# One kind of DMA at a time: transposes and GpSimd loads that wait for each other, in a Nyströmformer attention and SiLU layer kernel

## The chip, the core and the metric

One NeuronCore of a Trainium2 chip runs the whole program. The metric is the device time in microseconds of one execution. PE is TensorE, ACT ScalarE, DVE VectorE, POOL GpSimd, SP SyncE. PE has two clock levels, 1.2 and 2.4 GHz; the profile gives the granted clock as a share of the higher.

## The reference

Inputs q, k and v are 8 batches x 8 heads x 576 tokens x 64, in f32. Per head, 32 landmarks are means of 18 tokens each; three softmaxes follow, and an inverse by six Newton steps:

```python
q_lm = q.reshape(B, H, 32, 18, D).mean(axis=3)   # k_lm likewise
A = sm(q, k_lm); Bm = sm(q_lm, k_lm); C = sm(q_lm, k)
Z = Bm.transpose(0, 1, 3, 2) / (norm1(Bm) * norminf(Bm) + 1e-06)
for _ in range(6):
    Z = 2 * Z - Z @ Bm @ Z
x = A @ Z @ C @ v            # heads side by side: 4608 x 512
h = x @ w_in                 # 512 x 2048
out = (h * sigmoid(h)) @ w_out
```

## The kernel before, in words

The work goes batch by batch (8 batches, b = 0 to 7). A batch is cut into two groups of four heads (g = 0, 1), so that the 128 partitions hold four heads x 32 landmarks. What happens to one batch:

- **Loads** (`load_qk`, L361, and `load_v`, L369). k, q and v come from HBM in f32 and are cast to bf16 on the way, so GpSimd issues them (queue 0 of the profile): one DMA of 576 KB for k, one for q, three of 192 KB for v. Each of the tiles `qk` and `v` has two buffers.
- **Landmarks** (L504 to L515). From batch 2 on (`NPE = 2`), GpSimd adds up the 18 tokens in a tree, six instructions for k and six for q.
- **Transposes of q and k** (L470 to L477). Matmuls want head dimension on partitions. In batches 0 and 1 PE transposes; from batch 2 on the DMA does it: four `dma_start_transpose` per batch, `xt`, issued by SP (queue 1 of the profile), `qT<-qk`.
- **Softmaxes** (L535 to L688). Bm gives the Newton chain on DVE and PE; A gives `etn`; C gives `ce`. ACT computes all exponentials of a batch as one group, since it must change its function table between exp and SiLU.
- **Transposes of C** (L706 to L710). From batch 2 on two DMA transposes per batch, `ct<-ce`, also issued by SP. Then `cv` (L714) multiplies by v, `zt` and `m` (L743 to L771) fold in Z and w_in.
- **Layer 1** (`layer1`, L778): 16 blocks of two 512-column matmuls and two of sixteen 64-column ones, each followed by a SiLU on ACT. It writes `gm`, three buffers.
- **Layer 2** (`layer2`, L831): tiles of 16 matmuls of 512 columns, copied to `ost` (three buffers) by ACT or DVE, and stored by SP (`store_rows`, L857), on the same queue 1 as the transposes.

All instructions are put in order before the kernel is built: `Plan.run` (L59) simulates the five engines and one DMA queue with given durations, and takes at each free engine the ready operation of lowest `prio`. An operation with `dma=` us is queued behind the others on one modelled DMA (`dmaq`, L197) and is done `lag` later (1.9 us for loads, `XLAG` for transposes). What the plan yields is a fixed order for every engine; on the chip each engine goes through its list in order and waits where an operand isn't there yet. Stores and transposes stand in one list, SP's; loads and landmark additions in one list, POOL's. Nothing in the kernel before orders loads against transposes, except that a load into a `qk` buffer waits for the transposes that read that buffer two batches earlier (`p["qk_read"]`, L896), and v for `cv` two batches earlier (L897).

Of the kernel before, what the change touches and what calls it, by code (L numbers as in the profile page):

```python
# [17 lines left out]
class Op:  # L18


    def __init__(self, name, engs, emit, deps=(), prio=0.0, psum=0, cls=None, table=None,
                 tiled=False, dma=0.0, lag=None, group=None, crit=False):
        self.name, self.engs, self.emit, self.prio = name, engs, emit, prio
        self.deps = [d if isinstance(d, tuple) else (d, None) for d in deps if d is not None]
        self.psum, self.cls, self.table, self.tiled = psum, cls, table, tiled
        self.dma, self.lag, self.group, self.crit = dma, lag, group, crit
        self.unit = None
        self.margin = 0.0 if crit or engs[0][0] != "PE" else Plan.MARGIN
        self.slot = None
        self.readers = [0] * psum  # L30
        self.frees = []
        self.done = None
        self.left = 0
        self.users = []
# [218 lines left out]
def kernel(  # L253
# [9 lines left out]
    nc = tc.nc  # L263
# [11 lines left out]
    sc = 1.0 / float(Dh) ** 0.5  # L275
    SW = 128 + L
    NPE = 2
    XLAG = 3.5

    constp = ctx.enter_context(tc.tile_pool(name="constp", bufs=1))  # L280
    natp = ctx.enter_context(tc.tile_pool(name="natp", bufs=1))
# [66 lines left out]

    swdge = []

    def load(name, prio, us, issue, emit, deps=()):
        d = list(deps)
        if len(swdge) >= 8:
            d.append((swdge[-8], None))
        o = A(name, [("POOL", issue)], emit, d, prio, dma=us)
        swdge.append(o)
        return o

    qk_ops, v_ops, wi_ops, wo_ops = {}, {}, {}, {}

    def load_qk(b, prio, deps=()):  # L361
        for t, src in ((1, k), (0, q)):
            qk_ops[b, t] = load(
                f"ld{t}.{b}", prio + t * -0.1, 2.9, 0.75,
                lambda e, t=t, src=src: nc.gpsimd.dma_start(  # L365
                    out=qk_r[b % 2][:, t].rearrange("p g j d -> p g (j d)"),
                    in_=src[b].rearrange("(g h) (l j) d -> (h l) g (j d)", g=NG, l=L)), deps)

    def load_v(b, prio, deps=()):  # L369
        v_ops[b] = [load(  # L370
            f"ldv{a}.{b}", prio, 0.97, 0.6,
            lambda e, a=a: nc.gpsimd.dma_start(  # L372
                out=v_r[b % 2][a * L:(a + 1) * L, :, :],
                in_=v[b].rearrange("h (l a x) d -> a l h (x d)", l=L, a=VA)[a]), deps)
            for a in range(VA)]

    def load_w_in(f, prio):
# [53 lines left out]
    def attn(b):  # L431
# [12 lines left out]
        if on_pe:  # L444
            blocks = {}
            me["qk_read"] = []
            for t in (1, 0):
                todo = [(g, jp) for g in range(NG) for jp in range(JP)]
                for i in range(0, 18, 4):
                    part = todo[i:i + 4]  # L450

                    def tmm(e, t=t, part=part, key=(t, i)):
                        ps = bank(blocks[key])
                        for n, (g, jp) in enumerate(part):
                            mm(ps[:, n * 128:(n + 1) * 128],
                               qk[:, t, g, 2 * jp:2 * jp + 2, :].rearrange("p j d -> p (j d)"),
                               idb)
                    o = blocks[t, i] = A(f"tr{t}{i}.{b}", [("PE", mm_us(128, len(part)))], tmm,
                                         [qk_ops[b, t], cid], p0 + 7 + (1 - t) * 0.5, psum=1)
                    me["qk_read"].append(o)  # L460

                    def tcp(e, t=t, i=i, n=len(part), key=(t, i)):
                        copy(e, qT[:, t].rearrange("p g j x -> p (g j) x")[:, i:i + n, :],
                             bank(blocks[key])[:, 0:n * 128].rearrange("p (n x) -> p n x", x=128))
                    c = A(f"trc{t}{i}.{b}", either(128 * len(part)), tcp, [o], p0 + 8).reads(o)
                    for g, _ in part:
                        qt_ops.setdefault((t, g), []).append(c)
        else:
            me["qk_read"] = []
            for t in (1, 0):  # L470
                for g in range(NG):
                    qt_ops[t, g] = [A(
                        f"xt{t}{g}.{b}", [("SP", 0.1)],
                        lambda e, t=t, g=g: nc.sync.dma_start_transpose(  # L474
                            out=qT[:, t, g], in_=qk[:, t, g].rearrange("p j d -> p (j d)")),
                        [qk_ops[b, t]] + use, p0 + 5, dma=1.35, lag=XLAG)]
                    me["qk_read"] += qt_ops[t, g]  # L477


        lm_ops = {}  # L480
# [185 lines left out]
        for g in range(NG):  # L666
            ce, ct = ce_r[g], ct_r[g]

            def cm(e, g=g):
                for h in range(4):  # L670
                    for c in range(2):
                        mm(bank(me[f"C{g}"], c)[L * h:L * h + L, 0:HS],
                           lmT[64 * c:64 * c + 64, 0, g, L * h:L * h + L],
                           qT[64 * c:64 * c + 64, 1, g, :, L * h:L * h + L])
            me[f"C{g}"] = A(f"C{g}.{b}", [("PE", 0.24)], cm,
                            lmT_all + [(pb_op, -0.2)] + qt_ops[1, g], p0 + 18 + g,
                            psum=2, tiled=True)
            xs = []
            for c in range(2):
                def cx(e, g=g, ce=ce, c=c):  # L680
                    nc.scalar.activation(  # L681
                        out=ce[:, :, 0:VP].rearrange("p (i c) (a l) -> p c a i l", c=2, a=VA)[:, c],
                        in_=bank(me[f"C{g}"], c)[:, 0:HS].rearrange(
                            "p (a i l) -> p a i l", a=VA, l=L),
                        func=AF.Exp, scale=sc / J, accum_out=csum[:, 2 * g + c:2 * g + c + 1])
                xs.append(A(f"Cx{g}{c}.{b}", [("ACT", act_us(HS) + 0.1)], cx,
                            [me[f"C{g}"]] + prev.get("cts", []), p0 + 19 + g, table="exp",
                            group=grp).reads(me[f"C{g}"], c))  # L688
            me["csum", g] = xs
            if on_pe:  # L690
                ct_ops[g] = []
                for i0 in range(0, VI, 3):
                    def ctm(e, g=g, ce=ce, i0=i0):
                        ps = bank(me["ctm", g, i0])
                        for n in range(3):
                            mm(ps[:, n * 128:(n + 1) * 128], ce[:, i0 + n, :], idb)
                    o = me["ctm", g, i0] = A(f"ctm{g}{i0}.{b}", [("PE", mm_us(128, 3))], ctm,
                                             xs + [cid], p0 + 20, psum=1)
                    me["cts"].append(o)
                    ct_ops[g].append(A(  # L700
                        f"ctc{g}{i0}.{b}", either(384), lambda e, g=g, ct=ct, i0=i0: copy(
                            e, ct[:, i0:i0 + 3, :].rearrange("p i x -> p (i x)"),
                            bank(me["ctm", g, i0])[:, 0:384]), [o, prev.get("cv")],
                        p0 + 20).reads(o))
            else:
                ct_ops[g] = [A(f"ct{g}.{b}", [("SP", 0.1)], lambda e, ce=ce, ct=ct:  # L706
                               nc.sync.dma_start_transpose(
                                   out=ct, in_=ce.rearrange("p i x -> p (i x)")),
                               xs + [prev.get("cv")], p0 + 20, dma=1.3, lag=XLAG)]
                me["cts"] += ct_ops[g]  # L710

        wsb, zt = wsb_r[b % 2], zt_r[b % 2]
# [144 lines left out]
    def store_rows(b, js, ost, p0):  # L857
        n = len(js)
        step = js[1] - js[0] if n > 1 else 1
        nc.sync.dma_start(  # L860
            out=out[b * S:(b + 1) * S, :].rearrange("(l j) n -> j l n", j=J)
            [js[0]:js[-1] + 1:step],
            in_=ost[p0:p0 + n * L, :])
# [4 lines left out]
    def layer2_batch(b):  # L868
        l2_last["m", b] = []
        for c in range(4):  # L870
            js = [jof(x) for x in range(4 * c, 4 * c + 4)]

            def stores(ost, js=js):
                i = 0
                while i < 4:
                    n = 1
                    while i + n < 4 and js[i + n] == js[i] + 2 * n:
                        n += 1
                    store_rows(b, js[i:i + n], ost, i * L)
                    i += n  # L880
            l2_last["m", b] += layer2(
                lambda dc, c=c: gm_r[b % 3][:, dc, c * 128:(c + 1) * 128], lambda qt: gm_ops[b][4 * qt:4 * qt + 4],
                5000.0 + 100 * b + 10 * c, stores)
        if b % 2 == 1:
            def stores(ost):
                for bb in range(2):
                    store_rows(b - 1 + bb, [jof(16), jof(17)], ost, 64 * bb)
            l2_last["x", b // 2] = layer2(
                lambda dc: gx_r[(b // 2) % 2][:, dc, :], 
                lambda qt: [gx_ops[b - 1][qt // 2], gx_ops[b][qt // 2]],  # L890
                5000.0 + 100 * b + 40, stores)

    for b in range(B):
        if b >= 2:
            p = last[b - 2]
            load_qk(b, 100.0 * b - 150, p["qk_read"])  # L896
            load_v(b, 100.0 * b - 140, [p["cv"]])  # L897
        attn(b)
        layer1(b)
        layer2_batch(b)  # L900
# [4 lines left out]
    with tc.manual_schedule(engines={ET.PE, ET.Activation, ET.DVE, ET.Pool, ET.SP}):  # L905
        table = None
        for o, e, t, end, switch in order:
            if switch and o.table == "exp":
                nc.scalar.add_instruction(mybir.InstLoadActFuncSet(  # L909
                    act_func_set_id=EXP_SET, name=nc.get_next_instruction_name(),  # L910
                    engine=ET.Activation))
            o.emit(e)


PLAN_DUMP = None
# [30 lines left out]
```

## Time and profile before

| | us |
|---|---|
| runs shown | 340.24, 340.89, 344.27 (median 340.89) |
| the profiled execution | 343.25 |
| its span, first to last instruction | 341.5 |
| PE busy | 270.9 (79%) |
| ACT busy | 178.6 (52%) |
| mean granted PE clock | 0.904 |

The durations that the prediction uses come from the profiled execution, whose own time is 343.25 us, 1.75 us more than its span. "SPq" marks instructions of SP's queue: the time of a DMA instruction there is how long SP was held by it, not how long the data took.

### The profile page before, as it was taken

The numbers are of one execution on the slowest core, as the hardware profiler recorded it, in microseconds if no ns is written. First come the engines' busy times: TensorE is split into PE (matmuls) and PEld (weight loads), VectorE is DVE, ScalarE is ACT, GpSimd is POOL, SyncE is SP. The second block draws the span as 40 slices with busy tenths as digits, with TensorE's granted clock in tenths as the row PEclk, the third lists the DMA queues.
The fourth block names the chain that finished last, engine by engine and source line by source line (L and its number), as shares of the span: only waits on it lengthen the run. The fifth ranks groups of instructions, "written<-read, shape, count | busy, mean of one in ns | idle before, by whom it ended". The sixth has DMA issues, their size and how long they took to land.

```text
span 341.5 us, 5931 instructions
## 1 busy us (share of the span) xinstructions
PE 270.9 (79%) x2332; PEld 136.3 (40%) x2367; DVE 96.5 (28%) x258; ACT 178.6 (52%) x405; POOL 106.4 (31%) x133
## 2 busy tenths in 40 slices
PE   8999999269249924039999829999999999999960
PEld 6965554124014402014444314454444544444420
DVE  1774074202023423012236822306484000000000
ACT  1887982198300528006995644998589383121120
POOL 7266269471393484004995402000000000000000
PEclk9999999969866986558999976999999999999995
DMA  7999999999999994994739999104430120222221
GB/s 121 208 199 200 206 207 180 130 119 129 153 107 109 166 157 67 89 163 77 117 83 180 130 107 182 37 2 79 75 76 23 29 59 24 71 67 79 82 73 43
DMA packets 58147, 37.60 MB, mean 110 GB/s; under 512 B 39176, under 2 KB 49416, under 8 KB 58120
## 3 DMA queue, kind: packets, MB, share of 16 engines
q0 software_dynamic: 15232, 18.35, 38.8%
q1 hardware_dynamic: 42888, 18.88, 37.4%
q8 instruction: 18, 0.29, 0.4%
q14 instruction: 9, 0.07, 0.1%
HBM read 36.70 MB, written 9.44 MB: 135 GB/s over the span
## 4 chain that ended last, share of the span: by engine, by line
PE 60%; DMA 25%; ACT 5%; DVE 2%; issue 2%; POOL 1%; SPq 1%; ACTq 0%; POOLq 0%; DVEq 0%
PE ps L321 60%; DMA ct<-ce 11%; DMA out_dram<-ost 8%; DMA w_in_sb<-in_moe_w_in_dram 6%; ACT gm L798 2%; POOL qk L365 1%; DVE bbd L566 1%; DVE st L610 1%; ACT ce L681 1%; ACT ost L331 1%; POOL v L372 1%; ACT gx L820 0%; ACT L909 0%; ACT L798 0%; SPq L474 0%
## 5 line engine op out<-in xcount | busy, mean ns | idle before, releaser
L321 PE MATMUL ps<-w_out_sb,gm 128*128 128x512 bf16 x493 | 122.7, 390 | 6.8 <-ACT ost L331 4.8
L321 PE MATMUL ps<-etn,m 128*128 128x64 bf16 (+1 forms) x500 | 73.8, 297 | 10.6 <-ACT gm L798 8.6
L798 ACT ACTIVATE gm<-ps 128x512 bf16<-128x512 f32 x128 | 67.5, 633 | 27.2 <-remote 17.3
L321 PEld LDWEIGHTS <-gm 128*128 128x128 bf16 x512 | 49.0, 100 | 60.0 <-issue 12.4
L331 ACT COPY ost<-ps 128x512 f32<-128x512 f32 x27 | 15.8, 585 | 78.1 <-PE ps L321 51.0
L321 PEld LDWEIGHTS <-m 128*128 128x128 bf16 x512 | 33.2, 101 | 40.2 <-issue 17.4
L610 DVE SCALAR_TENSOR_TENSOR st<-st,ps 128x320 bf16<-128x320 bf16 (+3 forms) x54 | 21.6, 407 | 52.4 <-PE ps L321 50.0
L372 POOL DMA_DIRECT2D v<-in_v_dram x24 | 14.0, 588 | 59.8 <-PE ps L321 55.4
L506 POOL TENSOR_TENSOR sa<-qk 128x576 f32<-128x576 bf16 x24 | 30.6, 1295 | 3.7 <-DMA qk<-in_k_dram 2.8
L321 PE MATMUL ps<-v,ct 96*64 96x128 bf16 x192 | 9.4, 240 | 23.8 <-DMA ct<-ce 23.5
L333 DVE CAST m<-ps 128x512 bf16<-128x512 f32 x32 | 20.5, 684 | 10.0 <-PE ps L321 9.9
L506 POOL TENSOR_TENSOR sb<-sa 128x512 f32<-128x512 f32 (+1 forms) x24 | 21.4, 891 | 1.6
L331 ACT CAST m<-ps 128x512 bf16<-128x512 f32 x32 | 17.3, 603 | 5.5 <-PE ps L321 5.5
L321 PEld LDWEIGHTS <-ct 96*64 96x64 bf16 x192 | 6.6, 120 | 29.0 <-DMA ct<-ce 24.5
L321 PE MATMUL ps<-st 128*128 128x160 bf16 (+1 forms) x96 | 16.1, 245 | 1.1 <-DVE st L610 0.9
L638 ACT ACTIVATE et<-ps 128x288 bf16<-128x288 f32 x32 | 11.3, 417 | 10.4 <-PE ps L321 10.3
L321 PE MATMUL ps<-zer 128*128 128x256 bf16 x95 | 15.4, 308 | 1.1 <-DVE zer L399 1.1
L657 DVE TENSOR_TENSOR etn<-et,ln 128x576 bf16<-128x576 bf16 x16 | 13.8, 865 | 7.7 <-ACT ln L652 7.6
L681 ACT ACTIVATE ce<-ps 128x288 bf16<-128x288 f32 x32 | 12.7, 410 | 5.9 <-PE ps L321 5.9
L321 PE MATMUL ps<-w_out_sb,gx 128*128 128x512 bf16 x60 | 15.4, 380 | 0.2 <-issue 0.2
L321 PEld LDWEIGHTS <-st 128*128 128x128 bf16 x96 | 9.1, 107 | 13.5 <-issue 5.2
L321 PE MATMUL ps<-qT,lmT 64*32 64x288 bf16 x256 | 8.9, 297 | 6.0 <-DVE m L333 5.8
(68 smaller groups left out, 242.7 us busy)
## 6 DMA issues: line engine op xcount, KB each, us to landing
out_dram<-ost SPq DMA_DIRECT2D x24, 256.0 KB
qk<-in_k_dram POOLq DMA_DIRECT2D x8, 576.0 KB, 14.2
qk<-in_q_dram POOLq DMA_DIRECT2D x8, 576.0 KB, 16.3
v<-in_v_dram POOLq DMA_DIRECT2D x24, 192.0 KB, 12.3
w_out_sb<-in_moe_w_out_dram POOLq DMA_DIRECT2D x4, 512.0 KB, 10.5
out_dram<-ost SPq DMA_DIRECT2D x8, 192.0 KB
w_in_sb<-in_moe_w_in_dram POOLq DMA_DIRECT2D x4, 256.0 KB, 9.4
w_in_sb<-in_moe_w_in_dram POOLq DMA_DIRECT2D x8, 128.0 KB, 7.1
```

The costliest lines, as they stand in the source:

```text
L321: nc.tensor.matmul(out=out_ap, lhsT=lhsT, rhs=rhs, start=start, stop=stop, skip_group_check=True)
L331: nc.scalar.copy(out=out, in_=in_)
L333: nc.vector.tensor_copy(out=out, in_=in_)
L365: lambda e, t=t, src=src: nc.gpsimd.dma_start(out=qk_r[b % 2][:, t].rearrange("p g j d -> p g (j d)"), in_=src[b].rearrange("(g h) (l j) d ...
L372: lambda e, a=a: nc.gpsimd.dma_start(out=v_r[b % 2][a * L:(a + 1) * L, :, :], in_=v[b].rearrange("h (l a x) d -> a l h (x d)", l=L, a=VA)[ ...
L506: lambda e: nc.gpsimd.tensor_tensor(out=o_, in0=a_, in1=b_, op=OP.add),
L566: bbd_op = chain("bbd", 0.2, lambda: nc.vector.tensor_tensor(out=bbd, in0=bc(bmt, 4, 2), in1=bc(hmask, NG, 1), op=OP.mult), [bmt_op, prev. ...
L610: nc.vector.scalar_tensor_tensor(out=s2[:, g0:g1, lo:SW], in0=s[:, g0:g1, lo:SW], scalar=2.0, in1=ps[:, 0:NG * SW].rearrange("p (g x) -> p ...
L638: lambda e, g=g, et=et, c=c: nc.scalar.activation(out=et[:, c], in_=bank(me[f"A{g}"], c)[:, 0:HS], func=AF.Exp, scale=sc / J),
L657: nc.vector.tensor_tensor(out=etn[:, g, :], in0=et.rearrange("p c x -> p (c x)"), in1=ln.rearrange("p c x -> p (c x)"), op=OP.mult)
L681: nc.scalar.activation(out=ce[:, :, 0:VP].rearrange("p (i c) (a l) -> p c a i l", c=2, a=VA)[:, c], in_=bank(me[f"C{g}"], c)[:, 0:HS].rear ...
L798: lambda e, dc=dc, cell=cell: nc.scalar.activation(out=gm[:, dc, :], in_=bank(cell["o"]), func=AF.Silu),
```

## The change

Loads and transposes take turns. The four `xt` of batch b wait for the two `ct` of batch b-1 (in batch 2: for the last v load of batch 2). The loads of batch b+1 wait for the `xt` of batch b (from batch 3 on). The two `ct` of batch b wait for the last v load of batch b+1. The waits are real ones on the DMAs' semaphores (`add_manual_dep`) and known to the plan. So per batch the DMA does: `xt`(b), loads of b+1, `ct`(b), `xt`(b+1), and so on. Stores are in no turn. Besides, the plan's figures for a transpose become 1.42 us and a lag of 0.7 us (from 1.35 or 1.3, and 3.5), `load_v`'s priority moves next to `load_qk`'s, and the loads of batch b+1 are put to the plan within `attn(b)`.

```diff
-    XLAG = 3.5
+    XLAG = 0.7
-    def load(name, prio, us, issue, emit, deps=()):
-        d = list(deps)
+    def load(name, prio, us, issue, emit, deps=(), after=()):
+        d = list(deps) + list(after)
...
+        o.after = after
...
             me["qk_read"] = []
+            me["xts"] = []
+            gate = v_ops[b][-1:] if b == NPE else prev["cts"]
             for t in (1, 0):
                 for g in range(NG):
                     qt_ops[t, g] = [A(
...
-                        [qk_ops[b, t]] + use, p0 + 5, dma=1.35, lag=XLAG)]
+                        [qk_ops[b, t]] + use + gate, p0 + 5, dma=1.42, lag=XLAG)]
+                    qt_ops[t, g][0].after = gate
                     me["qk_read"] += qt_ops[t, g]
+                    me["xts"] += qt_ops[t, g]
+
+        if NPE <= b + 1 < B:
+            later_loads(b + 1)
...
-                               xs + [prev.get("cv")], p0 + 20, dma=1.3, lag=XLAG)]
+                               xs + [prev.get("cv")] + v_ops.get(b + 1, [])[-1:], p0 + 20, dma=1.42, lag=XLAG)]
+                ct_ops[g][0].after = v_ops.get(b + 1, [])[-1:]
...
+    def later_loads(b):
+        p = last[b - 2]
+        gate = last[b - 1]["xts"] if b > NPE else []
+        load_qk(b, 100.0 * b - 150, p["qk_read"], gate)
+        load_v(b, 100.0 * b - 149, [p["cv"]], gate)
+
     for b in range(B):
-        if b >= 2:
-            p = last[b - 2]
-            load_qk(b, 100.0 * b - 150, p["qk_read"])
-            load_v(b, 100.0 * b - 140, [p["cv"]])
         attn(b)
...
-            o.emit(e)
+            r = o.emit(e)
+            if o.dma:
+                o.ins = r.ins
+            for x in o.after:
+                tc.add_manual_dep(o.ins, x.ins.name, mybir.DependencyInfo(
+                    mybir.DependencyClass.Sync, mybir.DependencyReason.DATA),
+                    reason="one kind of transfer at a time")
```

## Rows read from the trace of the kernel before

**Rows 1.** The page: busy time of each engine; the group of warming matmuls.

```profile
PE 270.9 (79%) x2332; PEld 136.3 (40%) x2367; DVE 96.5 (28%) x258; ACT 178.6 (52%) x405; POOL 106.4 (31%) x133
...
L321 PE MATMUL ps<-zer 128*128 128x256 bf16 x95 | 15.4, 308 | 1.1 <-DVE zer L399 1.1
```

**Rows 2.** Windows: length, busy us (count) by engine, PEclk, DMA share, GB/s.

```profile
60.00:208.00 148.00, 93.15 (x813) 43.27 (x827) 43.25 (x107) 71.37 (x168) 71.08 (x81) 0.81 1.08 125
208.00:330.00 122.00, 120.37 (x887) 56.34 (x900) 25.68 (x71) 67.26 (x144) 0.00 (x0) 0.99 0.26 59
330.00:341.50 11.50, 0.00 (x0) 0.00 (x0) 0.00 (x0) 0.41 (x1) 0.00 (x0) 0.66 0.15 51
```

**Rows 3.** Waits from 60 to 208 us: total us, times, longest us.

```profile
PE ps L321 <- DMA ct<-ce: 23.5, 3, 17.5
...
ACT ost L331 <- DMA out_dram<-ost: 23.1, 3, 13.9
...
POOL qk L365 <- DMA qT<-qk: 19.8, 5, 11.7
...
PE ps L321 <- ACT gm L798: 8.6, 1, 8.6
...
PE ps L321 <- POOL lm L506: 6.8, 1, 6.8
...
PE ps L321 <- DVE m L333: 5.8, 1, 5.8
...
PE ps L321 <- ACT ost L331: 4.8, 1, 4.8
```

**Rows 4.** SP's own timeline: start us, us held, instruction, count.

```profile
46.25 12.51 SPq L474 DMA_TRANSPOSE qT<-qk  x2
...
121.70 11.83 SPq L707 DMA_TRANSPOSE ct<-ce  x1
...
135.38 8.26 SPq L707 DMA_TRANSPOSE ct<-ce  x1
...
178.02 2.85 SPq L707 DMA_TRANSPOSE ct<-ce  x2
180.96 5.66 SPq L474 DMA_TRANSPOSE qT<-qk  x4
```

**Rows 5.** DMA totals of the windows 30 to 46, 144 to 150, 149 to 156 us.

```profile
DMA packets 3056, 3.32 MB, mean 207 GB/s; under 512 B 128, under 2 KB 2679, under 8 KB 3053
...
DMA packets 840, 0.53 MB, mean 88 GB/s; under 512 B 667, under 2 KB 667, under 8 KB 840
...
DMA packets 5080, 1.28 MB, mean 183 GB/s; under 512 B 5068, under 2 KB 5068, under 8 KB 5080
```

**Rows 6.** Windows, two of six stretches at a low clock, and their sum.

```profile
71.00:76.50 5.50, 5.48 (x40) 2.26 (x40) 0.00 (x0) 4.94 (x10) 5.15 (x7) 0.70 1.36 96
93.90:98.00 4.10, 4.06 (x12) 1.67 (x13) 1.89 (x3) 0.00 (x0) 3.96 (x3) 0.50 2.46 144
...
sum 31.60, PE 29.68 PEld 13.68 DVE 8.94 ACT 13.87 POOL 17.89; mean PE 4.95 PEld 2.28 DVE 1.49 ACT 2.31 POOL 2.98
```

**Rows 7.** POOL's timeline, k and q of batch 7 issued: start us, us.

```profile
164.91 0.73 POOL L365 DMA_DIRECT2D qk<-in_k_dram  x1
165.64 0.71 POOL L365 DMA_DIRECT2D qk<-in_q_dram  x1
```

**Rows 8.** Loads, KB each and us from issue to landing: 121:133 (first), 164:177.

```profile
qk<-in_q_dram POOLq DMA_DIRECT2D x1, 576.0 KB, 26.1
...
qk<-in_k_dram POOLq DMA_DIRECT2D x1, 576.0 KB, 8.2
qk<-in_q_dram POOLq DMA_DIRECT2D x1, 576.0 KB, 10.3
```

More of the change, by code (lines that the diff above doesn't have):

```diff
@@ L27, in __init__ @@
         self.unit = None
+        self.after = ()
+        self.ins = None
         self.margin = 0.0 if crit or engs[0][0] != "PE" else Plan.MARGIN
@@ L359, with load_qk @@
     qk_ops, v_ops, wi_ops, wo_ops = {}, {}, {}, {}
-    def load_qk(b, prio, deps=()):
+    def load_qk(b, prio, deps=(), after=()):
         for t, src in ((1, k), (0, q)):
@@ L366, in load_qk, with load_v @@
                     out=qk_r[b % 2][:, t].rearrange("p g j d -> p g (j d)"),
-                    in_=src[b].rearrange("(g h) (l j) d -> (h l) g (j d)", g=NG, l=L)), deps)
-    def load_v(b, prio, deps=()):
+                    in_=src[b].rearrange("(g h) (l j) d -> (h l) g (j d)", g=NG, l=L)), deps, after)
+    def load_v(b, prio, deps=(), after=()):
         v_ops[b] = [load(
@@ L373, in load_v @@
                 out=v_r[b % 2][a * L:(a + 1) * L, :, :],
-                in_=v[b].rearrange("h (l a x) d -> a l h (x d)", l=L, a=VA)[a]), deps)
+                in_=v[b].rearrange("h (l a x) d -> a l h (x d)", l=L, a=VA)[a]), deps, after)
             for a in range(VA)]
@@ L859, in store_rows @@
         step = js[1] - js[0] if n > 1 else 1
-        nc.sync.dma_start(
+        return nc.sync.dma_start(
             out=out[b * S:(b + 1) * S, :].rearrange("(l j) n -> j l n", j=J)
@@ L878, in stores @@
                         n += 1
-                    store_rows(b, js[i:i + n], ost, i * L)
+                    r = store_rows(b, js[i:i + n], ost, i * L)
                     i += n
+                return r
             l2_last["m", b] += layer2(
@@ L886, in stores @@
                 for bb in range(2):
-                    store_rows(b - 1 + bb, [jof(16), jof(17)], ost, 64 * bb)
+                    r = store_rows(b - 1 + bb, [jof(16), jof(17)], ost, 64 * bb)
+                return r
             l2_last["x", b // 2] = layer2(
```

## The prediction

> **What bounds the kernel now.** The views were read in this order: the page, the windows by stage, the waits, SP's own timeline, the DMA totals of short windows.
>
> The page shows PE busy for 79% of the span [rows 1]. That share is a mean over two very different parts, so the windows come next. From 208 us to 330 us PE works 120.37 of 122 us, 98.7%, at a clock of 0.99: this part is bound by PE and nothing else. From 60 to 208 us PE works 93.15 of 148 us, at a mean clock of 0.81 [rows 2]. So 54.85 us of PE idle time lie in this middle part, and it is the only part with much to win.
>
> The waits of that part say what ended PE's gaps [rows 3]. The largest stand behind the transposes of C (23.5 us, one gap of 17.5). The other four rows name ACT, POOL and DVE, but those had waited themselves: ACT's copy into `ost` waited 23.1 us for earlier stores, and GpSimd's k and q loads 19.8 us for the transposes of q and k. Stores stand in SP's list among the transposes, so a transpose that holds SP holds the stores, these hold `ost`, that holds ACT, and ACT holds PE. The five rows for PE add up to 49.5 of the 54.85 us, and behind every one of them is a DMA transpose.
>
> SP's timeline shows why: the `ct` at 121.70 held SP for 11.83 us, the next one for 8.26. Yet at 178.02 two took 2.85 us together, and at 180.96 four `xt` took 5.66: 1.42 us each both times [rows 4]. The difference is what ran beside them. Between 121.70 and about 150 us the q load of batch 6 was in flight, and it took 26.1 us to land, where the same load at 165.64 took 10.3 [rows 7, 8]. The DMA totals say the same: loads alone moved 207 GB/s, transposes alone 183 (a few idle us among them), and 88 GB/s from 144 to 150 us, with both kinds in flight [rows 5]. So the two kinds don't merely share the engines; together they move less than half of what either moves alone.
>
> **The change, part by part.** All terms are for the profiled execution (span 341.5, time 343.25 us).
>
> *Removed: the idle time of the middle part.* If transposes take 1.42 us each, SP is held 2.85 us by a `ct` pair and 5.66 by the `xt` of a batch, and the gaps of [rows 3] have no cause. At most all 54.85 us go; the well-fed part still idles 1.3%, which on the 93 us of work left is about 1 us. I take -54. At the least nothing goes, if the slow DMA has another cause.
>
> *Removed: the low clock.* After each long gap PE came back at half clock. Six such stretches, 31.6 us together with 29.68 us of PE work, had clocks from 0.50 to 0.70 [rows 6]. At clock c a stretch T would have done its work in c x T, so 0.3 to 0.5 of 31.6 us is lost: 9.5 to 15.8. I take -13, as more of the six lie near 0.50. It goes only where the gaps go.
>
> *Added: the turns.* One batch's turns, from durations of undisturbed transfers: `xt` 5.66; loads of k and q from 164.91 to 165.64 + 10.3 = 175.94, so 11.0 us [rows 7, 8], and v, another 576 KB at 207 GB/s, 2.9; `ct` 2.85. Together 22.4 us, with handovers some 25 (an estimate: no row shows a load that waits for a transpose and nothing else). Against this stands PE's work for a batch: 270.9, less 15.4 of warming matmuls and 13 of low clock, over 8: 30.3 us [rows 1]. So the turns fit beside a batch's PE work with about 5 us to spare, and cost nothing by themselves.
>
> *Added: waits that the plan doesn't foresee.* The lists are fixed by a plan that takes a load turn to be 0.75 + 0.1 + 2 x 2.9 + 3 x 0.97 + 1.9 = 11.5 us; the rows say 13.9. Where the plan puts `ct` or the instructions after it right behind the loads' end, the engines wait 2.4 us more per batch. Behind the waiting `ct` on SP are `xt` and stores; behind these wait `ost`, ACT and DVE copies, and PE. GpSimd's loads that wait for `xt` hold back the landmark additions behind them. The bounds: nothing, if the 5 us of slack takes it, and 30 us, if each of six batches loses the 5 us of slack as well. I take 6 x 2.4 = 15, the full lateness, because on PE's in-order list a late operand is made up only from slack behind it.
>
> *Moved:* the first `xt` (at 46.25 us in SP's timeline [rows 4]) now wait for the last v of batch 2, and the k and q loads of batch 3 wait for them. In exchange these four transposes no longer share the DMA: the first two alone held SP for 12.51 us. I count it as nothing; PE has batch 1 to work on there. The new lag of 0.7 us lets the plan use transposes 2.8 us earlier; clean transposes bear that out, so nothing again.
>
> *Not touched:* stores beside transposes or loads. The four `xt` of 180.96 ran with stores around them at full pace [rows 4].
>
> The sum: 341.5 - 54 - 13 + 15 = 289.5, plus the 1.75 outside the span: 291. The median of the runs shown is 2.4 us under the profiled execution (340.89 to 343.25), so on its scale the forecast is **289 us**. The middle part becomes PE-bound like the last one. The case's own range is 276 (no lateness) to 303 (30 us of it).
>
> The Trainium skill speaks against the change. "DMA: Bandwidth & Descriptors", section "Issuing engines are not separate DMA queues", says that DMAs of all issuing engines run on the same 16 engines and interleave; its "Rules for kernel authors" add that a transpose next to ordinary DMAs needs nothing. If interleaving lost nothing, turns would win nothing. The trace disagrees, with 88 GB/s for both against 207 and 183 for each.
>
> **The rivals.**
>
> *The turns bound the middle part.* A batch then takes P us, the period of the turns, from the first `xt` (about 50 us) to the last `ct` six periods later; behind it lie one batch's PE work (30) and the 11.5 us after PE's end [rows 2], about 42. The span is 92 + 6P. At 25 it is less than PE's own bound, at 33 it equals the forecast. If exponentials, loads and transposes overlap only in part, P = 36 and the time is 308 + 1.75 = 310. For it: six operations of a loop in strict order, and SP's list. Against it: the 5 us of slack.
>
> *Slower: the turns and ACT's work run one after the other.* `ct`(b) in SP's list waits for v of b+1; a store behind it can't leave; ACT's copy into `ost` waits for that store, and SiLUs and exponentials queue behind the copy, as ACT's waits of 23.1 us already show [rows 3]. Then ACT's 178.6/8 = 22.3 us per batch [rows 1] add to the turns' 22.4 + 0.5: P = 45.2, span 363, time 365. It decides from P = 41.6 on, where 92 + 6P reaches the present span. Against it: three `ost` buffers, and a plan that knows the waits.
>
> *No change: mixing isn't the cause.* Slow transposes could be slow from stores or from the queue's depth, and turns leave both. Then gaps and low clock stay, and the time is about 343 again (341 on the median's scale). Against it: the full pace at 180.96 us, beside stores but no loads. The Trainium skill's rule, above, would give this.
>
> *Half a cure.* The gaps behind `ct` go, but those that began with a store stuck on SP (8.6, 5.8 and 4.8 us [rows 3]) stay, as SP now waits for loads instead, with 5 us of low clock: 291 + 24 = 315.
>
> **How the numbers follow.** Forecast (PE-bound, about 289): 0.58. Turns bound it (310): 0.19. Half a cure (315): 0.09. No change: 0.06. Slower (365): 0.08. About 2% is what a measurement here can tell from no change. The first three are faster by over 2%: 0.86; same 0.06; slower 0.08. The range runs from 276, the forecast without lateness, to 325, past the two middle cases with some lateness; left out are the last two cases and little more.
>
> **What would show it right or wrong.** Right: each transpose holds SP for about 1.4 us; no window with both queues in flight has half the bandwidth; loads land in 8 to 11 us; PE's waits for `ct<-ce` fall from 23.5 to a few us; from 60 us on PE is above 90% busy with a clock near 1. The lateness shows as short waits of PE or ACT once per batch. Wrong: transposes that still take 5 us and more with no load in flight (mixing isn't the cause); gaps of PE once per batch at the `ct` with SP waiting for v (the turns bound it); ACT waiting for stores while SP stands at a `ct` (the slower case).

## The result, and the profile after

The changed kernel takes 326.62 us (median of 4 runs, 326.54 to 327.44) against 342.58 us for the kernel before in the same comparison: a ratio of 0.956, with a 95% interval of 0.948 to 0.964. It is faster, as forecast, but by 4.4% where 15% were forecast, and the time lies just outside the range (276 to 325). The profiled execution took 326.66 us, its span is 324.9 us. Here and below, the times are medians over all runs, while ratios leave out runs that took over 1.5% longer than the fastest of the same kernel.

The page and two windows of the changed kernel answer to [rows 1, 2] (length, busy us and count by engine, PEclk, DMA share, GB/s):

```profile
PE 271.2 (83%) x2367; PEld 135.5 (42%) x2367; DVE 97.3 (30%) x258; ACT 178.1 (55%) x405; POOL 106.2 (33%) x133
```

```profile
60.00:235.00 175.00, 135.21 (x1254) 63.47 (x1255) 60.74 (x159) 104.11 (x245) 74.54 (x87) 0.89 0.76 128
235.00:313.50 78.50, 78.50 (x480) 35.82 (x476) 8.88 (x19) 33.65 (x65) 0.00 (x0) 0.96 0.18 49
313.50:324.90 11.40, 0.04 (x1) 0.00 (x0) 0.00 (x0) 0.59 (x1) 0.00 (x0) 0.59 0.16 59
```

PE's busy time is the same (270.9 and 271.2 us), so the whole gain is idle time: span less PE's busy time went from 70.6 to 53.7 us. The part in which PE starves still exists: from 60 to 235 us it is idle for 175 - 135.21 = 39.8 us, where 54.85 us stood before (60 to 208 us), and its mean clock there is 0.89. Behind 235 us PE is the bound again.

The waits of the changed kernel, whole span (us in total, times, longest), answer to [rows 3]:

```profile
POOL qk L368 <- DMA qT<-qk: 48.7, 5, 12.1
...
POOL sa L516 <- DMA qk<-in_k_dram: 34.2, 6, 7.6
...
PE ps L323 <- POOL lm L516: 18.9, 4, 8.5
PE ps L323 <- DMA ct<-ce: 18.7, 5, 6.9
```

The waits of ACT and DVE for stores are gone. PE's wait for `ct<-ce` fell only from 23.5 to 18.7 us, now in five pieces, and its wait for the landmarks rose from 6.8 to 18.9. These come from the chain of turns: GpSimd waits 48.7 us for transposes before it may load, then 34.2 us for k to land, then adds up the landmarks for which PE stands.

SP's timeline shows the turns (answering to [rows 4]), and POOL's gives the start of three load turns ([rows 7]):

```profile
81.52 2.58 SPq L717 DMA_TRANSPOSE ct<-ce  x2
84.19 0.54 SPq L871 DMA_DIRECT2D out_dram<-ost  x1
85.80 8.08 SPq L479 DMA_TRANSPOSE qT<-qk  x4
93.98 5.04 SPq L871 DMA_DIRECT2D out_dram<-ost  x4
115.83 2.75 SPq L717 DMA_TRANSPOSE ct<-ce  x2
118.67 1.14 SPq L871 DMA_DIRECT2D out_dram<-ost  x2
120.18 9.80 SPq L479 DMA_TRANSPOSE qT<-qk  x4
142.16 0.56 SPq L871 DMA_DIRECT2D out_dram<-ost  x1
144.43 3.36 SPq L717 DMA_TRANSPOSE ct<-ce  x2
149.97 5.51 SPq L479 DMA_TRANSPOSE qT<-qk  x4
155.59 10.63 SPq L871 DMA_DIRECT2D out_dram<-ost  x5
179.71 2.58 SPq L717 DMA_TRANSPOSE ct<-ce  x2
...
207.69 4.47 SPq L717 DMA_TRANSPOSE ct<-ce  x2
```

```profile
97.89 0.73 POOL L368 DMA_DIRECT2D qk<-in_k_dram  x1 [11.70 <-DMA qT<-qk]
...
132.58 0.74 POOL L368 DMA_DIRECT2D qk<-in_k_dram  x1 [11.89 <-DMA qT<-qk]
...
158.14 0.74 POOL L368 DMA_DIRECT2D qk<-in_k_dram  x1 [7.51 <-DMA qT<-qk]
```

From one `ct` turn to the next it takes (207.69 - 81.52)/4 = 31.5 us, not 25. The long pieces have stores at their head. The `xt` after two stores (120.18) hold SP for 9.80 us, those at 149.97, with no store just ahead, 5.51. The load turn with four stores at its start runs from 97.89 to the `ct` at 115.83, 17.9 us; the one with five from 158.14 to 179.71, 21.6; the one with none ahead of it from 132.58 to 144.43, 11.9. So no load is in flight beside these transposes, and they are slow all the same.

The DMA view of the changed kernel from 119 to 133 us, around the 9.80 us, in 40 slices (busy share in tenths, then GB/s), says what kind of slow this is:

```profile
DMA  9411010111396991111111999999944999940100
GB/s 214 84 18 18 12 12 28 44 50 63 77 114 159 139 61 53 53 47 59 47 41 24 226 281 290 205 291 239 177 17 86 292 281 286 275 82 0 47 0 0
```

For several us the DMA engines are one tenth busy and move 12 to 77 GB/s, while transposes wait. That is no crowding: most engines have nothing to do. Packet counts of two short windows show who was moving. A transpose's packets are of 256 bytes, a store's of 2 KB (one output row). The first line is 124 to 126 us, the second 126.5 to 128.5:

```profile
DMA packets 55, 0.10 MB, mean 52 GB/s; under 512 B 5, under 2 KB 5, under 8 KB 55
```

```profile
DMA packets 1888, 0.48 MB, mean 238 GB/s; under 512 B 1887, under 2 KB 1887, under 8 KB 1887
```

While a store's 50 rows pass, 5 packets of transposes pass; once the store is through, the transposes run at 238 GB/s.

The kernel before has this picture in part in the window 121 to 133 us, where its `ct` held SP for 11.83 us, right behind four stores:

```profile
DMA  9999973396377999999999499222232222222222
GB/s 117 98 100 157 168 168 63 73 105 98 104 142 178 199 206 213 214 212 160 128 97 111 86 73 81 66 58 73 58 79 65 58 73 65 65 73 58 79 65 65
```

```profile
117.46 4.14 SPq L860 DMA_DIRECT2D out_dram<-ost  x4
```

Up to about 128 us, with loads in flight, the engines are mostly nine tenths busy; from there on it is two tenths and 58 to 79 GB/s, much the same as both kernels show where stores run alone, at the end of the span (0.15 and 51 GB/s in [rows 2], last window; 0.16 and 59 above). The window 144 to 150 us, from which the prediction read loads against transposes, has such a stretch too. From 148.5 to 149.5 us nothing but store rows passed, while SP was held by four `xt` (143.75 to 153.74 us):

```profile
DMA packets 24, 0.05 MB, mean 49 GB/s; under 512 B 0, under 2 KB 0, under 8 KB 24
```

### The profile page after: what moved, and what is told of

It is laid out like the page before. It is cut to its first block, busy times and chain, and to the rows that moved or that the text cites. A ratio compares the mean times of both kernels' runs of the same rounds, so it can differ in the third digit from the quotient of the medians.

```text
span 324.9 us, 5951 instructions
## 1 busy us (share of the span) xinstructions
PE 271.2 (83%) x2367; PEld 135.5 (42%) x2367; DVE 97.3 (30%) x258; ACT 178.1 (55%) x405; POOL 106.2 (33%) x133
## 4 chain that ended last, share of the span: by engine, by line
PE 48%; DMA 32%; POOL 7%; SPq 5%; issue 2%; ACT 1%; DVE 1%; POOLq 0%; ACTq 0%
PE ps L323 48%; DMA ct<-ce 9%; DMA w_in_sb<-in_moe_w_in_dram 6%; DMA qk<-in_k_dram 6%; DMA v<-in_v_dram 6%; DMA qT<-qk 5%; SPq L479 5%; POOL sa L516 2%; POOL qk L368 2%; POOL v L375 1%; POOL sb L516 1%; ACT ce L691 1%; POOL lm L516 1%; DVE etn L667 1%; SPq L717 0%
## 5 line engine op out<-in xcount | busy, mean ns | idle before, releaser
L323 PE MATMUL ps<-etn,m 128*128 128x64 bf16 (+1 forms) x512 | 75.9, 302 | 0.0
L323 PEld LDWEIGHTS <-gm 128*128 128x128 bf16 x512 | 47.4, 98 | 53.2 <-issue 3.7
L333 ACT COPY ost<-ps 128x512 f32<-128x512 f32 x25 | 14.7, 587 | 58.7 <-PE ps L323 58.6
L516 POOL TENSOR_TENSOR sa<-qk 128x576 f32<-128x576 bf16 x24 | 30.4, 1286 | 34.7 <-DMA qk<-in_k_dram 34.2
L620 DVE SCALAR_TENSOR_TENSOR st<-st,ps 128x320 bf16<-128x320 bf16 (+3 forms) x54 | 21.6, 408 | 50.9 <-PE ps L323 48.4
L323 PE MATMUL ps<-v,ct 96*64 96x128 bf16 x192 | 10.0, 251 | 18.7 <-DMA ct<-ce 18.7
L335 DVE CAST m<-ps 128x512 bf16<-128x512 f32 x31 | 19.8, 686 | 8.5 <-PE ps L323 8.4
L368 POOL DMA_DIRECT2D qk<-in_k_dram x8 | 6.0, 747 | 49.9 <-DMA qT<-qk 48.7
L323 PE MATMUL ps<-idb,lm 128*128 128x128 bf16 x32 | 4.6, 235 | 19.0 <-POOL lm L516 18.9
L333 ACT CAST m<-ps 128x512 bf16<-128x512 f32 x33 | 17.9, 616 | 2.6 <-PE ps L323 2.6
L335 DVE COPY ost<-ps 128x512 f32<-128x512 f32 x11 | 7.6, 690 | 29.5 <-PE ps L323 29.5
L323 PE MATMUL ps<-zer 128*128 128x256 bf16 x95 | 14.9, 301 | 1.1 <-DVE zer L402 1.1
L323 PE MATMUL ps<-st 128*128 128x160 bf16 (+1 forms) x96 | 15.4, 237 | 0.0
```

What stands on the lines that cost most here:

```text
L323: nc.tensor.matmul(out=out_ap, lhsT=lhsT, rhs=rhs, start=start, stop=stop, skip_group_check=True)
L333: nc.scalar.copy(out=out, in_=in_)
L335: nc.vector.tensor_copy(out=out, in_=in_)
L368: lambda e, t=t, src=src: nc.gpsimd.dma_start(out=qk_r[b % 2][:, t].rearrange("p g j d -> p g (j d)"), in_=src[b].rearrange("(g h) (l j) d ...
L516: lambda e: nc.gpsimd.tensor_tensor(out=o_, in0=a_, in1=b_, op=OP.add),
L620: nc.vector.scalar_tensor_tensor(out=s2[:, g0:g1, lo:SW], in0=s[:, g0:g1, lo:SW], scalar=2.0, in1=ps[:, 0:NG * SW].rearrange("p (g x) -> p ...
```

## The experiments

Two theories were set against each other. **S**: the stores stretch the turns, since a store uses few DMA engines. **L**: the turns are long by themselves, through handovers and a plan that puts them too early.

**e1: stores cut by rows, in the changed kernel.** A store writes up to four blocks of 32 output rows, so its slowest dimension is 1 to 4. Now each block is a DMA of its own:

```diff
-        return nc.sync.dma_start(
-            out=out[b * S:(b + 1) * S, :].rearrange("(l j) n -> j l n", j=J)
-            [js[0]:js[-1] + 1:step],
-            in_=ost[p0:p0 + n * L, :])
+        for i, j in enumerate(js):
+            r = nc.sync.dma_start(
+                out=out[b * S:(b + 1) * S, :].rearrange("(l j) n -> j l n", j=J)[j],
+                in_=ost[p0 + i * L:p0 + (i + 1) * L, :])
+        return r
```

> The changed kernel, each store of an ost tile cut into one DMA per 32 rows of the output (64 KB each) instead of runs of up to four. Theory S (stores that take no turn stretch the turns: they move some 70 GB/s at a DMA share of 0.2, and the transposes behind them in SP's queue and the loads beside them wait): the four xt hold SP 5.7 to 6.5 us instead of 8 to 10, a load turn lands within 11 to 13 us of its first issue instead of 18 to 21, and the time falls from 326.6 to 300 to 315 us. Theory L (the stretch comes from the handovers and from a plan that puts the turns too early, stores have no part): the time stays within 2% of 326.6 us and the xt still hold SP 8 us or more.

Measured: 292.93 us against 340.11 for the kernel before (ratio 0.869, 0.859 to 0.879). S holds, by more than it said. SP's timeline and PE's waits of e1:

```profile
84.83 5.59 SPq L479 DMA_TRANSPOSE qT<-qk  x4
...
107.21 2.54 SPq L717 DMA_TRANSPOSE ct<-ce  x2
...
192.74 2.54 SPq L717 DMA_TRANSPOSE ct<-ce  x2
```

```profile
PE ps L323 <- POOL lm L516: 11.0, 3, 5.1
PE ps L323 <- DMA ct<-ce: 4.7, 3, 2.4
```

The `xt` hold SP 5.6 to 6.8 us in all turns, stores or not, and the turns come every 28 us ((192.74 - 107.21)/3 = 28.5). Loads are quicker as well: in four load turns v lands 9.3 to 11.2 us after its issue (median of three DMAs), against 14.9 and 17.7 us in the change's turns with four and five stores at their start.

**e2: the same cut in the kernel before, no turns.**

> The kernel before, with the stores cut in the same way and nothing else. If loads beside transposes are the chief loss (the theory of the prediction), single transposes still hold SP 5 us and more while loads are in flight, and the time stays at 330 to 343 us. If slow stores in SP's queue were the chief loss all along, the time falls below 320 us without any turns.

Measured: 297.63 us (0.881, 0.869 to 0.893). So the cut alone, without any turns, takes some 40 us from the kernel before, over twice what the change took. Of the first outcome, the long holds beside loads came true, the time didn't. Four `xt` beside loads, once of two such times (the other took 16.25 us):

```profile
69.29 16.48 SPq L474 DMA_TRANSPOSE qT<-qk  x4
```

These long holds cost less now: PE's idle time from 60 to 208 us is 22.2 us (125.80 of 148 us busy) instead of 54.85. Stores still wait behind them. ACT waits 26.6 us in all for stores, more than the 23.1 before, but in nine pieces of at most 6.6 us instead of three of up to 13.9.

**e3: the changed order without the waits on the chip** (the loop with `add_manual_dep` taken out; the plan still knows the waits).

> The changed kernel's order of instructions on every engine, without the added waits on the chip (the plan still knows them). If the waits do the work, loads and transposes overlap again wherever an engine runs ahead of the plan, and the time goes back towards 335 to 343 us. If the order alone keeps them mostly apart, it stays within 2% of 326.6 us, or is a few us faster since no handover is waited for: 318 to 333 us.

Measured: 332.84 us, with runs from 326.1 to 341.7: too wide to say whether the waits help here. The median lies at the edge of the second outcome, the slowest run in the first, the fastest at the change's own time.

**e4: the new plan figures alone, in the kernel before.**

> The kernel before with the new plan figures for a transpose alone (1.42 us and a lag of 0.7 us instead of 1.35 or 1.3 and 3.5). The prediction counted this at nothing: 335 to 346 us, with the same long holds of SP by transposes. If the figures are part of the gain, below 334 us.

Measured: 338.01 us (1.003, 0.992 to 1.014): no change, as counted.

**e5: stores cut by columns.** Two DMAs of 256 columns each, the same one to four blocks:

```diff
+        w = DMODEL // 2
+        for c in range(2):
+            r = nc.sync.dma_start(
+                out=out[b * S:(b + 1) * S, c * w:(c + 1) * w].rearrange("(l j) n -> j l n", j=J)
+                [js[0]:js[-1] + 1:step],
+                in_=ost[p0:p0 + n * L, c * w:(c + 1) * w])
```

> The changed kernel, each store cut into two DMAs by columns (256 of 512 columns each, the same runs of up to four 32-row blocks). These are smaller stores, as in the cut by rows, but each still has one to four blocks as its slowest dimension. If the cut by rows helped because a store then spreads over all DMA engines (theory spread), this one doesn't help: 322 us or more, DMA share still 0.2 to 0.3 where a store runs alone. If it helped because stores became smaller (theory size), this gets at least a third of the 34 us: 315 us or less.

Measured: 318.57 us (0.938, 0.931 to 0.945). Neither outcome: some 8 us better than the change, a quarter of what the cut by rows gave. The share where stores run alone stays at 0.23. Why it gains 8 us is open.

**e6: stores uncut, but issued from ACT's queue** (`nc.scalar.dma_start` in place of `nc.sync.dma_start`).

> The changed kernel with its stores uncut, but issued from ACT's queue instead of SP's. If transposes are slow because they stand behind stores in the same hardware queue, the four xt hold SP 5.7 to 6.5 us again, and the time falls to 295 to 312 us (ACT pays some 0.56 us for each of 48 stores, 27 us in all, most of it beside its waits). If the stores slow the DMA engines themselves, whatever their queue, the xt still hold SP 8 us and more in turns that have stores beside them, and the time stays above 318 us.

Measured: 351.13 us (1.036, 1.026 to 1.046), worse than before. The `xt` beside which ACT issued stores were still slow:

```profile
164.57 10.70 SPq L479 DMA_TRANSPOSE qT<-qk  x4
```

```profile
165.97 0.56 ACTq L871 DMA_DIRECT2D out_dram<-ost  x1
169.40 1.84 ACTq L871 DMA_DIRECT2D out_dram<-ost  x2
```

The first four `xt` (at 51.87 us) were held 11.82 us beside ACT's stores, those at 134.44, with none issued in the six us before them or beside them, 5.55. So it isn't the order within SP's queue that makes transposes slow beside a store; stores of another queue do the same to them. How much of the 24 us over the change is ACT's own holding at stores wasn't separated.

**e7: stores cut by rows, changed order, no waits on the chip.**

> The changed kernel with stores cut by rows and without the added waits on the chip (the plan's order stays). Beside the 292.9 us with the waits this says what the waits themselves are worth once stores are quick. If loads beside transposes cost, as the prediction held, the time is 296 to 306 us. If the waits only cost handovers now, it is 285 to 291 us.

Measured: 291.91 us (0.862, 0.857 to 0.868), as with the waits (292.93; intervals overlap), and just between the two ranges expected. Loads beside transposes cost no time that can be measured here, though five of the six groups of `xt` held SP 7.6 to 11.2 us, against 5.6 to 6.8 in e1. Its DMA total from 79 to 91 us, where four `xt` held SP for 11.16 us with k, q and v loads in flight:

```profile
DMA packets 5233, 2.51 MB, mean 209 GB/s; under 512 B 4437, under 2 KB 4683, under 8 KB 5233
```

209 GB/s, as much as either kind alone [rows 5]. Two such windows of e2 had 132 GB/s, so mixing isn't free everywhere, but it doesn't halve the bandwidth as the prediction read from [rows 5].

**e8: stores cut by rows, and the plan's lags set nearer to the trace** (2.2 us instead of 0.7 for a transpose, 2.7 instead of 1.9 for a load).

> The changed kernel with stores cut by rows, and a plan that takes transposes to land 2.2 us (not 0.7) and loads 2.7 us (not 1.9) after their data time, nearer to what its trace shows. If what is left of PE's idle time (17.8 us in gaps) is lateness against the plan, PE's waits for lm and ct (15.7 us together) fall by half and the time to 283 to 290 us. If it is the period of the turns itself, the time stays within 1% of 292.9 us.

Measured: 275.20 us (0.812, 0.808 to 0.816), 18 us under e1 and below the expected 283 to 290. The lateness against the plan was worth more than its visible gaps: with these gone, PE's busy time fell as well, from 267.7 to 257.5 us, at a mean clock of 1.00 instead of 0.96. Page, a window and a wait of e8:

```profile
PE 257.5 (94%) x2339; PEld 132.8 (49%) x2374; DVE 102.9 (38%) x262; ACT 180.0 (66%) x407; POOL 106.2 (39%) x133
```

```profile
60.00:235.00 175.00, 167.39 (x1488) 80.70 (x1508) 71.88 (x172) 124.17 (x282) 73.17 (x85) 1.00 0.76 140
```

```profile
PE ps L323 <- POOL lm L516: 1.5, 3, 0.9
```

PE's clock is 1.00, and it idles 7.6 us where the change left 39.8. This is the fastest version of the study.

**e9: stores cut by rows, at most two blocks per DMA.** These are smaller stores, but with a slowest dimension of 2 or 1.

> The changed kernel, each store cut by rows again, but into DMAs of at most two 32-row blocks (128 KB) instead of one. Theory spread (a store uses as many DMA engines as its slowest dimension divides into, so two here, and sixteen for a single block of 32 rows): the DMA share where stores run alone is near 2/16 = 0.12, stores become the bound, and the time rises to 370 us or more. Theory size (smaller stores are quicker): between 293 and 326 us.

Measured: 361.20 us (1.072, 1.056 to 1.088). These are two runs only. Not quite the 370 us, but slower than the uncut stores by 35 us, where smaller stores should have helped. Stores alone, 40 slices: the changed kernel (270 to 310 us), e1 (250 to 285) and e9 (310 to 350):

```profile
DMA  2220002175211222211132222223222222222222
```

```profile
DMA  5550000555500006233530155550002555500025
GB/s 148 143 136 23 0 0 16 134 150 148 143 9 0 0 19 152 63 84 91 138 80 0 40 134 136 141 150 0 0 0 63 136 129 136 136 0 0 0 70 143
```

```profile
DMA  1111111131131111111111111131141111111111
GB/s 66 53 49 51 51 51 51 51 109 51 55 105 51 51 51 49 53 49 51 51 51 51 51 51 51 51 109 51 49 111 49 51 51 51 51 51 51 51 51 51
```

With up to four blocks a store keeps two tenths of the engines busy, with two blocks one tenth and mostly a flat 51 GB/s (the mean share is 0.16, since single blocks are among them), with single blocks of 32 rows five tenths at 130 to 150 GB/s, with pauses in between. The start and length of each packet in the traces say it more directly. In these windows four packets of SP's queue are in flight at once for 51% of the time in the changed kernel, two for 85% in e9, and ten to sixteen for 27% in e1. The Trainium skill states the rule, "DMA: Bandwidth & Descriptors", section "Why a DMA increments its semaphore by 16 and not by 1": the number of engines is the largest up to 16 that divides the slowest dimension (the outermost larger than 1) of both sides. 4 of 16 is 0.25 and 2 of 16 is 0.12; the trace agrees with both, by share and by packets in flight. For a block of 32 rows the rule gives all 16, which the packets reach for moments only; the share stays at five tenths.

**e10: stores uncut, the lags of e8.**

> The changed kernel with its stores uncut, and the plan's lags at 2.2 us for transposes and 2.7 us for loads (0.7 and 1.9 in the change). This says what of the shortfall was lateness against the plan and what the stores. If lateness can be planned away even with slow stores, the time falls to 305 to 318 us. If the slow stores set the period of the turns, it stays within 2% of 326.6 us.

Measured: 311.94 us (0.925, 0.916 to 0.935), 15 us under the change. Its `xt` hold SP as long as the change's (8.2 to 9.2 us), its turns are longer still ((258.22 - 80.58)/5 = 35.5 us from `ct` to `ct`), and PE's waits for `ct` are nearly gone, those for the landmarks not:

```profile
84.85 9.21 SPq L479 DMA_TRANSPOSE qT<-qk  x4
```

```profile
PE ps L323 <- POOL lm L516: 19.2, 7, 5.4
PE ps L323 <- DMA ct<-ce: 2.9, 2, 1.7
```

So lateness can be planned away with slow stores too, in part. The lags that the change planned with, 0.7 us for transposes (new with it) and 1.9 us for loads, kept it from part of its gain. e8 and e10 alter both at once, so what each is worth wasn't separated.

**e11: e8 without the waits on the chip.**

> The 275.2 us version (stores cut by rows, lags 2.2 and 2.7) without the added waits on the chip. If turns on the chip are worth nothing once the order is right: within 1% of 275.2 us. If loads beside transposes still cost: 279 us or more.

Measured: 277.67 us over all six runs, 276.0 over the three that the ratio counts (0.818, 0.809 to 0.827): within 1% of e8, the intervals overlap. The waits themselves are worth nothing that can be told, once stores are cut.

**e12: the kernel before with stores cut by rows and the load lag of e8** (transposes were planned with 3.5 us there already).

> The kernel before (no turns, transposes planned with 3.5 us of lag) with stores cut by rows and loads planned to land 2.7 us after their data time instead of 1.9. If honest lags alone make the gain of the 275.2 us version: 275 to 285 us. If the turns in the plan, which keep the real DMA close to the planned one, are needed: 290 to 300 us, as without the new lag (297.6).

Measured: 303.37 us over all six runs, 298.35 over the two that the ratio counts (0.886, 0.872 to 0.899), the same as e2. The load lag alone gives nothing. e11, whose waits on the chip are missing as well, is some 22 us faster. It has the turns in its plan, a transpose lag of 2.2 instead of 3.5 us, and v planned next to k and q; these three weren't separated. With the change's own lags such an order was worth only some 5 us (e7 against e2).

## Why the prediction failed, point by point

**The cause of the slow transposes.** The step that failed is the reading "the two kinds don't merely share the engines; together they move less than half of what either moves alone". The window at 88 GB/s had store rows in flight too, and low DMA shares, which a view of GB/s alone doesn't tell from crowding. What the runs show in its place: uncut stores, which occupy few DMA engines, hold up the transposes and loads beside them. e2 takes some 40 us from the kernel before with the cut of the stores and no turns, and e7 shows 209 GB/s with loads and transposes in flight. Something of the mixture remains, in the 16 us holds and 132 GB/s of e2, but not "less than half". The prediction also set aside the Trainium skill's rule that "A transpose next to ordinary DMAs needs nothing" ("DMA: Bandwidth & Descriptors", section "Rules for kernel authors"). It stands in a row on corrupted data and says nothing of time. For time, e7 and e11 agree with it where stores are cut; beside the uncut stores of e6 it doesn't hold.

**"Not touched: stores beside transposes or loads."** Wrong, and the largest error. The one sample at full pace (180.96 us in [rows 4]) had no store just ahead of it on SP. Where stores stood just ahead, the four `xt` held SP 7.7 to 9.8 us, and load turns with stores at their start took 18 to 22 us instead of 12. The rival "mixing isn't the cause" named the stores, at a chance of 0.06, but concluded that nothing would change.

**The turns: 25 us a batch, with 5 us to spare.** Mis-sized: 31.5 us, against PE's 30.3. Besides the stores, the handovers were too small. From the end of the last `xt` on SP to the next k issue it took 158.14 - 155.48 = 2.7 us behind the quickest `xt` turn; the estimate had 2.6 us for all handovers of a batch. With the stores cut, the period was 28. But the period alone isn't what cost the change its gain: e10's turns took 35.5 us, and it is 15 us faster than the change.

**Lateness against the plan: +15.** The term was of the right kind. e10 measures what better lags win back with slow stores, 14.7 us; e8 against e1 17.7 us. But the prediction let it come from the load turn alone and counted the shorter transpose lag at nothing, which holds in the kernel before (e4), while the change's gaps added up to 39.8 us: the whole turn was late, not only the loads. The plan's figure for stores was too hopeful as well, in both kernels: it books an `ost` tile with `dma=0.65`, while 256 KB at the 70 GB/s that stores reach alone (270 to 310 us) take some 3.7 us, an estimate from these two. No run alters that figure.

**Idle time and low clock: -54 and -13.** They came to -17 (70.6 to 53.7 us over the span) and to nothing (PE busy 270.9 and 271.2 us). In e8, with stores cut and later lags, they did go: 7.6 us idle from 60 to 235 us, a clock of 1.00, and 275.2 us, close to the 276 that the prediction gave as the case without lateness. (That 276 is on the scale of the profiled execution, like its 291; on the scale of the forecast of 289 and of the upper end of 303 it is 274.) The bound by PE's work was sound; the change didn't reach it.

**The rivals.** "The turns bound the middle part" (310 us) is nearest to what happened, but its formula fails here: with P = 31.5 it gives a span of 281 us. It counts 42 us behind the last `ct`, one batch of PE's work and the end; in the change 324.9 - 231.4 = 93.5 us lay behind it, with 78.5 us of PE's work behind 235 us alone. With the lags of e8 and e10 PE kept up: 42.7 and 49.5 us lay behind the last `ct`, and with their P of 30.5 ((228.43 - 76.08)/5) and 35.5 us the formula gives 275 and 305 us, against spans of 273.7 and 310.3. "Slower" failed where it was to be checked: ACT's wait for stores went from 23.1 us to none in the list.

Why the change gains its 4.4% isn't shown. With stores cut, the order without the waits gives as much as with them (e7, e11). With slow stores, e3 leaves open whether the waits add to it, and e4 shows that the new figures alone give nothing in the kernel before.

## What to carry to other kernels

When transfers are slow, read the DMA share beside the GB/s. Here low GB/s at a full share was crowding (e2, 132 GB/s), and low GB/s at a share of 0.1 to 0.3 with work pending was a store on few engines, which others waited for. Look at the outermost dimension of each DMA before ordering transfers against each other: stores with 32 there instead of 1 to 4 were worth 34 to 40 us here, twice what the turns gave. And where a fixed order is planned, take lags from the trace of the kernel as it runs: a plan that was 1.5 us too hopeful for transposes and 0.8 for loads cost 15 to 18 us here.

## What the runs showed of the hardware that was not expected

Uncut stores, issued from ACT, slowed the transposes of SP's queue as well (e6: four `xt` took 10.70 and 11.82 us), so a queue of their own doesn't free them. That a transpose needs the very engines which the store occupies fits the packet counts, in which transposes stop while a store's rows pass, but the traces don't name the engine of a packet. Cutting the same bytes into smaller DMAs made the kernel 35 us slower with two blocks each (e9) and 34 us faster with one (e1). The end of the span shows it by itself: from PE's last matmul to the end it took 11.4 us with uncut stores, and in e8, with 64 KB stores on their way, 273.7 - 268.8 = 4.9 us.
